# Convolution taps on GpSimd: block 1 off TensorE, block 2 and the 64 last channels of blocks 2 and 3 off VectorE

## The chip, the cores and the metric

The kernel runs on one core of a Trainium2 chip. The metric is device time in microseconds (us) of one launch; lower is better. Five engines work side by side, each with its own queue that it empties in order: TensorE (PE in the rows, with its weight loads as PEld), VectorE (DVE), ScalarE (ACT), GpSimd (POOL) and SyncE (SP), which here issues nearly all transfers. An instruction waits until the semaphores that it names are high enough, and everything behind it on its engine waits with it.

## What is computed

Tokens (2 sequences of 4096, 192 channels) go through a causal convolution of 7 taps along the sequence, whose weights are a softmax over the taps and shared by the 24 channels of a head, then through two layers of the same form with different activations:

```python
out[b, s, c] = sum_k softmax(weight)[head(c), k] * x_pad[b, s + k, c]      # 7 taps
h = x @ w_in;  g = where(h >= 1, h, where(h <= -1, 0, (h + 1)**2 / 4));  x = g @ w_out
h = x @ w_in2; g = h * sigmoid(1.702 * h);                               out = g @ w_out2
```

with 192 x 2048 and 2048 x 192 weights in each layer.

## The kernel before, in words

Activations lie channels by tokens. The 8192 tokens are cut into 16 blocks of T = 512 tokens; a block has 128 first channels (tile `xt0`, part 0) and 64 last channels. The last channels of two neighbouring blocks share one tile of 128 partitions (`xt1`, part 1), so the convolution of part 1 is done for blocks 2j and 2j+1 at once. Matrix products run in fp32r with each operand split in a high and a low half: `split` (L72 to L74) lets ACT copy the high half and DVE subtract it to get the low one. The names are `xah`, `xal` for the halves of the 128 first channels of a block, `xb` for both halves of the last 64, `ghi`, `glo` for the halves of a hidden tile, `wt` for the weights.

The weights come as fp64 words (`raw`) and are turned into fp32 halves on the chip by `weight_ops` (L101): per tile of 128 hidden units, ACT makes `wa` (L117), DVE takes bits (L118) and joins them (L122) into `wd`, ACT copies the high half (L127), DVE makes the low halves (L131, L132). Layer 1 has 16 such tiles, f = 0 to 15.

Work is cut into units (phase, f), one hidden tile of one block and layer each, taken in an order written out by hand (`units`): f = 0 to 3 of block 0, then of block 1, then 4 to 7 of block 0, and so on, then block 2, and so on. A step issues the first product of unit u on PE (`gemm1`, L237, five matmuls), its activation on ACT and DVE (`act_a`, L265: two ACT instructions and one DVE instruction for layer 1), the split of the unit before (`act_b`, L279), and the second product of the unit four steps back (`gemm2`, L300, five matmuls). The first 48 steps run this way; after them two units are run together on the two halves of the PE array (`both`). Everything else is hung on steps by the dictionary `plan`: `at(step, op)` appends, and `beside(step)` emits it behind the step's own instructions. So every engine's order is fixed when the program is built.

The convolution is done in three ways in the kernel before.

- `conv_taps` (L148): seven DVE instructions of 128x512, the first a multiply (L152), the others a multiply-add (L153). Block 0's first channels (`cva`, before step 0) and all of blocks 2 to 15 go this way. For the pair j = 1 (blocks 2 and 3) one DVE instruction is hung on each of steps 10 to 25: seven taps of block 2's first channels, `put_a` (its split), seven taps of part 1 (`cvb`), `put_b`.
- `conv_on_pe` (L163): seven diagonal matrices of 128x128 (`diag`) are made, and seven fp32 matmuls add the taps up in PSUM. Part 1 of blocks 0 and 1 goes this way, with diagonals from ACT, into `cb_ps`.
- The same with diagonals from GpSimd: block 1's 128 first channels, into `ca_ps`. Its seven matmuls are hung on steps 0 to 2 behind `gemm1`; the split into `xah`, `xal` follows at step 2, and step 4 is the first that reads them.

The pool `o_p` (tag `o`, two buffers) holds the diagonals here, and output tiles much later.

Of the kernel before, what the change touches and what calls it, by code (L numbers as in the profile page):

```python
# [8 lines left out]
F32 = mybir.dt.float32  # L9
# [6 lines left out]
P = 128  # L16
T = 512
# [3 lines left out]
def kernel(  # L21
# [21 lines left out]
    nc = tc.nc  # L43
# [104 lines left out]
    def conv_taps(part, t, c):  # L148
        def tap(k):
            w, x = taps[:, part, k : k + 1], t[:, k : k + T]  # L150
            if k == 0:
                return lambda: nc.vector.tensor_scalar_mul(c, x, w)  # L152
            return lambda: nc.vector.scalar_tensor_tensor(c, x, w, c, op0=ALU.mult, op1=ALU.add)  # L153

        return [tap(k) for k in range(K)]

    def warm_up():

        w = bank(7, "warm")
        for _ in range(9):  # L160
            nc.tensor.matmul(w[:, 0:P], ident, ident, start=True, stop=True)
# [12 lines left out]
    def put_a(i, c):  # L174
        split(c, *x1[i][:2])
# [5 lines left out]
    def put_b(i, c):  # L181

        b, halved = i % B, phases.index((1, i)) * NF >= WHOLE
        t = x1[i][2 + (b if halved else 0)]
        hi, lo = (t[0:DB], t[DB:P]) if b == 0 else (t[DB:P], t[0:DB])
        split(c[b * DB : (b + 1) * DB], hi, lo)
        if halved:
            swap_halves(x1[i][3 - b], t)

    def conv_ops(j):  # L190

        ta, tb = xt[0, B * j], xt[1, j]
        ca = cv_p.tile([P, T], F32, tag="cva", name="cva")
        cb = cv_p.tile([P, T], F32, tag="cvb", name="cvb", bufs=1)
        x1[B * j] = new_xs()
        ops = conv_taps(0, ta, ca) + [lambda: put_a(B * j, ca)]
        ops += conv_taps(1, tb, cb) + [lambda: put_b(B * j, cb)]
        st = {}

        def begin():  # L200
            st["c"] = cv_p.tile([P, T], F32, tag="cva", name="cva")
            x1[B * j + 1] = new_xs()
            st["ops"] = conv_taps(0, xt[0, B * j + 1], st["c"])
            put_b(B * j + 1, cb)

        ops.append(begin)
        ops += [lambda: st["ops"].pop(0)() for _ in range(K)] + [lambda: put_a(B * j + 1, st["c"])]
        return ops
# [215 lines left out]
    def conv_at(j):  # L424
        first, second = (unit_at[phases.index((1, B * j + k)), 0] for k in range(B))
        ops = []
        at(first - 30, lambda: fetch_x((0, B * j), (1, j), (0, B * j + 1)))
        at(first - 22, lambda: ops.extend(conv_ops(j)))
        for k in range(2 * (K + 1)):
            at(first - 22 + k, lambda: ops.pop(0)())  # L430
        for k in range(K + 2):
            at(second - 16 + k, lambda: ops.pop(0)())

    with tc.manual_schedule():
        nc.sync.dma_start(taps, taps_in)
# [11 lines left out]
        for i in range(B):  # L447
            x1[i] = new_xs()
        ca = cv_p.tile([P, T], F32, tag="cva", name="cva")
        cb_ps, ca_ps = bank(3, "cb_ps"), bank(2, "ca_ps")  # L450
        a0 = conv_taps(0, xt[0, 0], ca)
        b_ops = conv_on_pe(1, xt[1, 0], cb_ps, ident, nc.scalar.mul)
        a1 = conv_on_pe(0, xt[0, 1], ca_ps, ident, nc.gpsimd.tensor_scalar_mul)
        for op in b_ops:
            op()

        ws = [weight_ops(1, f, raw.pop((1, f))) for f in range(CH - 1)]
        order = a0[0:3] + ws[0][0:1] + a0[3:5] + ws[0][1:3] + a0[5:7] + ws[0][3:4] + ws[1][0:1]
        order += [lambda: put_a(0, ca)] + ws[1][1:2] + [lambda: put_b(0, cb_ps)] + ws[1][2:] + ws[2]
        for op in order:  # L460
            op()
        fetch_w(1, 3)
        for k, op in enumerate(weights_at(1, 3)):
            at(k // 2, op)
        for k, op in enumerate(a1):
            at((k + 2) // 3, op)
        at(1, lambda: put_b(1, cb_ps))
        at(2, lambda: put_a(1, ca_ps))

        def convert_at(n, f, steps):  # L470
            at(steps[0] - 3, lambda: fetch_w(n, f))
# [108 lines left out]
```

## Time and profile before

| | us |
|---|---|
| median of 3 runs | 1138.7 (1138.65 to 1138.96) |
| the profiled execution, whole | 1138.51 |
| its span, first to last instruction | 1136.7 |
| PE busy in the span | 1127.7 (99%) |
| ACT busy | 823.0 (72%) |
| DVE busy | 713.6 (63%) |
| POOL busy | 6.7 (1%) |

The shares are means over the span. They say that PE is nearly always at work, but a PE row's end is modelled, so a PE that waits briefly between two matmuls can still look busy; there the distance between the starts of two matmuls tells more. The beginning (up to about 80 us) is different from the rest: there the weights of layer 1 are converted and the convolutions of the first blocks are done.

### The profile page before, as it was taken

What the parts mean: (1) busy time and instruction counts of PE and PEld (TensorE: products, weight loads), DVE (VectorE), ACT (ScalarE), POOL (GpSimd) and SP (SyncE); (2) the same over time, 40 slices, a digit from 0 to 9 for tenths busy, and PEclk for the clock granted to TensorE, in tenths of its full rate; (3) what the DMA queues carried; (4) which work ended last, traced back from release to release, by engine and by line L of the source; (5) the groups of instructions that cost most, each with busy time, mean ns of one, the idle gap of its engine ahead of it and who ended that gap; (6) DMA issues with size and microseconds to landing.
All of it is one profiled execution on the core that took longest, in us unless ns stands there. A gap on an engine that the chain in (4) does not pass through costs nothing.

```text
span 1136.7 us, 22822 instructions
## 1 busy us (share of the span) xinstructions
PE 1127.7 (99%) x9324; PEld 927.1 (82%) x9324; DVE 713.6 (63%) x1152; ACT 823.0 (72%) x1468; POOL 6.7 (1%) x13
## 2 busy tenths in 40 slices
PE   9999999999999999999999999999999999999998
PEld 5878888888888888888888888888888888888886
DVE  7998765675557756476564756647566575655532
ACT  7989875867758677686776768677586776868654
POOL 2000000000000000000000000000000000000000
PEclk9999999999999999999999999999999999999999
DMA  5321420100001000010000100010000100000000
GB/s 176 124 65 43 123 76 11 57 10 25 10 11 43 17 18 10 11 43 20 15 19 12 33 20 15 20 43 1 20 15 20 44 1 20 15 20 15 11 15 14
DMA packets 16680, 36.40 MB, mean 32 GB/s; under 512 B 2497, under 2 KB 2753, under 8 KB 16577
## 3 DMA queue, kind: packets, MB, share of 16 engines
q1 hardware_dynamic: 16432, 34.82, 10.4%
q8 instruction: 73, 1.20, 0.5%
q14 instruction: 31, 0.25, 0.1%
q10 hardware_dynamic: 144, 0.13, 0.0%
HBM read 21.05 MB, written 6.29 MB: 24 GB/s over the span
## 4 chain that ended last, share of the span: by engine, by line
PE 94%; DVE 3%; ACT 2%; issue 1%; DMA 0%; SPq 0%
PE acc L361 46%; PE h L361 42%; PE acc L315 3%; PE h L250 3%; DVE glo L74 1%; DVE a L274 1%; PE ca_ps L170 1%; DVE wd L122 0%; DVE cva L153 0%; DMA raw<-in_w_dram 0%; ACT a L273 0%; ACT a L272 0%; ACT wa L117 0%; ACT wt L127 0%; DVE wt L131 0%
## 5 line engine op out<-in xcount | busy, mean ns | idle before, releaser
L361 PE MATMUL acc<-ghi,wt 64*128 64x512 f32 x2772 | 835.1, 386 | 0.0
L361 PE MATMUL h<-xah,wt 64*128 64x512 f32 x1848 | 713.6, 386 | 0.0
L361 PE MATMUL acc<-glo,wt 64*128 64x512 f32 x1848 | 678.0, 386 | 0.0
L361 PEld LDWEIGHTS acc<-ghi,wt 64*128 64x128 f32 x2772 | 468.5, 184 | 53.9 <-ACT ghi L73 0.3
L74 DVE TENSOR_TENSOR glo<-a,ghi 128x512 fp32r<-128x512 f32 x512 | 341.3, 688 | 232.9 <-ACT ghi L73 223.6
L361 PEld LDWEIGHTS acc<-glo,wt 64*128 64x128 f32 x1848 | 340.0, 184 | 36.5 <-DVE glo L74 0.8
L361 PEld LDWEIGHTS h<-xah,wt 64*128 64x128 f32 x1848 | 340.0, 184 | 36.2 <-issue 0.4
L361 PE MATMUL h<-xal,wt 64*128 64x512 f32 x924 | 356.8, 386 | 0.0
L73 ACT CAST ghi<-a 128x512 fp32r<-128x512 f32 x512 | 301.3, 614 | 26.2 <-DVE a L274 25.7
L274 DVE SCALAR_TENSOR_TENSOR a<-h,a 128x512 f32<-128x512 f32 x256 | 176.8, 690 | 159.7 <-ACT a L273 159.4
L276 ACT ACTIVATE a<-h 128x512 f32<-128x512 f32 x256 | 150.8, 596 | 153.9 <-PE h L361 146.0
L361 PE MATMUL h<-xb,wt 64*128 64x512 f32 x693 | 230.9, 386 | 0.0
L361 PE MATMUL h<-xc,wt 64*128 64x512 f32 x693 | 230.7, 386 | 0.0
L272 ACT ACTIVATE a<-h 128x512 f32<-128x512 f32 x256 | 151.0, 590 | 53.0 <-PE h L361 52.3
L361 PEld LDWEIGHTS h<-xal,wt 64*128 64x128 f32 x924 | 170.0, 184 | 17.9
L273 ACT ACTIVATE a<-a 128x512 f32<-128x512 f32 x256 | 161.8, 632 | 8.2
L361 PEld LDWEIGHTS h<-xc,wt 64*128 64x128 f32 x693 | 127.5, 184 | 17.9
L361 PEld LDWEIGHTS h<-xb,wt 64*128 64x128 f32 x693 | 127.4, 184 | 9.0
L153 DVE SCALAR_TENSOR_TENSOR cva<-xt,taps,cva 128x512 f32<-128x512 f32 x90 | 67.2, 747 | 1.3
L250 PE MATMUL h<-xah,wt 128*128 128x512 f32 x100 | 40.5, 405 | 2.6 <-DVE wt L131 2.6
L315 PE MATMUL acc<-ghi,wt 128*128 128x512 f32 x150 | 42.4, 390 | 0.0
L315 PEld LDWEIGHTS acc<-ghi,wt 128*128 128x128 f32 x150 | 28.1, 188 | 6.2 <-issue 0.4
(61 smaller groups left out, 455.3 us busy)
## 6 DMA issues: line engine op xcount, KB each, us to landing
raw<-in_w_dram SPq DMA_DIRECT2D x32, 448.0 KB, 3.4
xc<-xb SPq DMA_DIRECT2D x44, 128.0 KB, 2.2
xt<-in_xa_dram SPq DMA_DIRECT2D x16, 259.0 KB, 3.5
out_dram<-o SPq DMA_DIRECT2D x15, 256.0 KB, 2.0
out_dram<-o SPq DMA_DIRECT2D x17, 128.0 KB, 2.3
xt<-in_xb_dram SPq DMA_DIRECT2D x8, 259.0 KB, 3.2
xb<-xc SPq DMA_DIRECT2D x14, 128.0 KB, 2.2
out_dram<-o ACTq DMA_DIRECT2D x1, 128.0 KB, 1.8
```

The source lines that it names most:

```text
L73: nc.scalar.copy(hi, src)
L74: nc.vector.tensor_sub(lo, src, f32(hi))
L153: return lambda: nc.vector.scalar_tensor_tensor(c, x, w, c, op0=ALU.mult, op1=ALU.add)
L170: return lambda: nc.tensor.matmul(c, d[:, k], t[:, k : k + T], start=k == 0, stop=k == K - 1)
L250: nc.tensor.matmul(h, w, r, start=j == 0, stop=j == len(prods) - 1)
L272: nc.scalar.activation(a, h, AF.Relu, bias=0.5, scale=0.5)
L273: nc.scalar.activation(a, a, AF.Square)
L274: nc.vector.scalar_tensor_tensor(a, h, 1.0, a, op0=ALU.max, op1=ALU.min)
L276: nc.scalar.activation(a, h, AF.Gelu_apprx_sigmoid)
L315: nc.tensor.matmul(acc, w, r, start=id(acc) in fresh, stop=last and ends[id(acc)] == k)
L361: mm = nc.tensor.matmul(banks[n], w, r, start=n in fresh, stop=ends.get(n) == k)
```

## The change

GpSimd gets a convolution of its own, `conv_taps_aside`: for each tap a multiply by the tap's weight and an add, where the multiply may be done by ACT. Block 1's first channels are multiplied by ACT (seven instructions, put between the weight instructions ahead of step 0) and added up by GpSimd (six adds), in SBUF; its seven matmuls on PE and its seven diagonals go. For j = 1, block 2's first channels and part 1 of blocks 2 and 3 are both multiplied and added by GpSimd (14 multiplies, 12 adds); block 3's first channels stay on DVE. The products lie in buffers `y` of the pool `o_p`.

```diff
+    def conv_taps_aside(part, t, c, mul=nc.gpsimd.tensor_scalar_mul):
+        def tap(k):
+            w, x = taps[:, part, k : k + 1], t[:, k : k + T]
+
+            def op():
+                if k == 0:
+                    mul(c, x, w)
+                else:
+                    y = o_p.tile([P, T], F32, tag="o", name="y")
+                    mul(y, x, w)
+                    nc.gpsimd.tensor_add(c, c, y)
+
+            return op
+
+        return [tap(k) for k in range(K)]
...
-        ops = conv_taps(0, ta, ca) + [lambda: put_a(B * j, ca)]
-        ops += conv_taps(1, tb, cb) + [lambda: put_b(B * j, cb)]
+        conv = conv_taps_aside if j == 1 else conv_taps
+        ops = conv(0, ta, ca) + [lambda: put_a(B * j, ca)]
+        ops += conv(1, tb, cb) + [lambda: put_b(B * j, cb)]
...
-        at(first - 30, lambda: fetch_x((0, B * j), (1, j), (0, B * j + 1)))
-        at(first - 22, lambda: ops.extend(conv_ops(j)))
-        for k in range(2 * (K + 1)):
-            at(first - 22 + k, lambda: ops.pop(0)())
+        if j == 1:
+            steps = [*range(4, 4 + K), 17, *range(5 + K, 5 + 2 * K), 25]
+            at(1, lambda: fetch_x((0, B * j), (1, j)))
+            at(20, lambda: fetch_x((0, B * j + 1)))
...
-        cb_ps, ca_ps = bank(3, "cb_ps"), bank(2, "ca_ps")
+        cb_ps = bank(3, "cb_ps")
+        ca1 = cv_p.tile([P, T], F32, tag="cva", name="cva")
...
-        a1 = conv_on_pe(0, xt[0, 1], ca_ps, ident, nc.gpsimd.tensor_scalar_mul)
+        a1 = conv_taps_aside(0, xt[0, 1], ca1, nc.scalar.mul)
...
-        order += [lambda: put_a(0, ca)] + ws[1][1:2] + [lambda: put_b(0, cb_ps)] + ws[1][2:] + ws[2]
+        order += a1[0:2] + [lambda: put_a(0, ca)] + a1[2:3] + ws[1][1:2] + [lambda: put_b(0, cb_ps)] + a1[3:4] + ws[1][2:3]
+        order += a1[4:6] + ws[1][3:] + ws[2][0:1] + a1[6:] + ws[2][1:]
...
-        for k, op in enumerate(a1):
-            at((k + 2) // 3, op)
...
-        at(2, lambda: put_a(1, ca_ps))
+        at(2, lambda: put_a(1, ca1))
```

The splits of block 2 stay hung on steps 17 and 25. The fetch of its inputs moves from step 2 to step 1, and that of block 3's first channels to step 20.

On ACT, ahead of step 0, this stands in the program before (behind the diagonals; `Pool_49` and its like are the engines' semaphores, `DMAHW` those of transfers):

```order
L117 ACTIVATE wa<-raw 128x448 [waits DMAHW4_49]
L73 CAST xah<-cva 128x512 [waits DVE_49]
L73 CAST xb<-cb_ps 64x512 [waits PE_49]
L127 CAST wt_88<-wd 128x448 [waits DVE_49]
L117 ACTIVATE wa<-raw 128x448 [waits DMAHW6_49,Activation_49]
L127 CAST wt_88<-wd 128x448 [waits DVE_49]
L272 ACTIVATE a<-h_201 128x512 [waits PE_49]
```

In the changed program the same place on ACT reads:

```order
L117 ACTIVATE wa<-raw 128x448 [waits DMAHW4_49]
L163 ACTIVATE cva<-xt,taps 128x512 [waits DMAHW5_49]
L166 ACTIVATE y<-xt,taps 128x512
L73 CAST xah<-cva 128x512 [waits DVE_49]
L166 ACTIVATE y<-xt,taps 128x512 [waits Pool_49]
L73 CAST xb<-cb_ps 64x512 [waits PE_49]
L166 ACTIVATE y<-xt,taps 128x512 [waits Pool_49]
L127 CAST wt_88<-wd 128x448 [waits DVE_49]
L166 ACTIVATE y<-xt,taps 128x512
L166 ACTIVATE y<-xt,taps 128x512 [waits Pool_49]
L117 ACTIVATE wa<-raw 128x448 [waits DMAHW6_49]
L166 ACTIVATE y<-xt,taps 128x512 [waits Pool_49]
```

Seven multiplies have come between the weight instructions and the splits of block 0, and four of the six that write `y` wait for GpSimd.

On GpSimd, from the making of the identity matrix to the end, this is the program before:

```order
masks.py:197 MEMSET ident 128x128
masks.py:199 ISA
masks.py:199 AFFINE_SELECT ident<-ident 128x128
L167 TENSOR_SCALAR diag<-ident,taps 128x128 x7
L573 UNCONDITIONAL_BRANCH
L573 ISA
```

The changed program has this on GpSimd from the same place on (the last pair of rows then goes on alike to six adds, and again to six for `cvb`):

```order
masks.py:199 AFFINE_SELECT ident<-ident 128x128
L167 TENSOR_TENSOR cva<-cva,y 128x512 x6
L163 TENSOR_SCALAR cva<-xt,taps 128x512
L166 TENSOR_SCALAR y<-xt,taps 128x512
L167 TENSOR_TENSOR cva<-cva,y 128x512
L166 TENSOR_SCALAR y<-xt,taps 128x512
L167 TENSOR_TENSOR cva<-cva,y 128x512
```

Seven narrow multiplies have gone, and 32 instructions of 512 columns have come.

On DVE, in steps 10 to 12, the program before reads (`a` is the activation, `h` the hidden tile in PSUM):

```order
L274 SCALAR_TENSOR_TENSOR a<-h_452,a 128x512
L74 TENSOR_TENSOR glo<-a,ghi 128x512
L131 TENSOR_TENSOR wt_88<-wd,wt_88 128x384
L132 TENSOR_TENSOR wt_88<-wd,wt_88 128x64
L122 SCALAR_TENSOR_TENSOR wd<-wa,wd 128x448
L152 TENSOR_SCALAR cva<-xt,taps 128x512
L274 SCALAR_TENSOR_TENSOR a<-h_483,a 128x512
L74 TENSOR_TENSOR glo<-a,ghi 128x512
L118 TENSOR_SCALAR wd<-raw 128x448
L153 SCALAR_TENSOR_TENSOR cva<-xt,taps,cva 128x512
```

In the changed program DVE has there:

```order
L291 SCALAR_TENSOR_TENSOR a<-h_476,a 128x512
L74 TENSOR_TENSOR glo<-a,ghi 128x512
L131 TENSOR_TENSOR wt_88<-wd,wt_88 128x384
L132 TENSOR_TENSOR wt_88<-wd,wt_88 128x64
L122 SCALAR_TENSOR_TENSOR wd<-wa,wd 128x448
L291 SCALAR_TENSOR_TENSOR a<-h_503,a 128x512
L74 TENSOR_TENSOR glo<-a,ghi 128x512
L118 TENSOR_SCALAR wd<-raw 128x448
```

One convolution instruction a step has gone from DVE; the others stand in their old order.

## Rows read from the trace of the kernel before

**Rows 1.** The page: engines over the span, and chain that ended last.
```profile
PE 1127.7 (99%) x9324; PEld 927.1 (82%) x9324; DVE 713.6 (63%) x1152; ACT 823.0 (72%) x1468; POOL 6.7 (1%) x13
...
PE 94%; DVE 3%; ACT 2%; issue 1%; DMA 0%; SPq 0%
```

**Rows 2.** Stretches: us, busy (instructions) of PE, PEld, DVE, ACT, POOL, clock, DMA, GB/s.
```profile
24.00:40.00 16.00, 16.00 (x71) 13.24 (x71) 14.36 (x31) 15.46 (x30) 0.00 (x0) 1.00 0.59 195
40.00:60.00 20.00, 18.97 (x84) 15.38 (x83) 19.20 (x39) 17.43 (x33) 0.00 (x0) 1.00 0.31 93
60.00:80.00 20.00, 18.40 (x81) 14.72 (x80) 19.95 (x40) 17.11 (x33) 0.00 (x0) 1.00 0.21 69
```

**Rows 3.** PE in order of time, around two waits: start, us, what, idle before.
```profile
57.25 0.61 PE L315 MATMUL acc<-glo,wt 128*128 128x512 f32 x2
58.90 0.50 PE L250 MATMUL h<-xah,wt 128*128 128x512 f32 x1 [1.03 <-DVE wt L131]
...
76.75 0.73 PE L315 MATMUL acc<-glo,wt 128*128 128x512 f32 x2
79.08 0.50 PE L250 MATMUL h<-xah,wt 128*128 128x512 f32 x1 [1.60 <-DVE wt L131]
```

**Rows 4.** The chain that ended last: start, us, what.
```profile
16.10 2.58 PE ca_ps L170 x6
...
83.92 1.13 PE h L250 x5
85.06 1.13 PE acc L315 x5
```

**Rows 5.** ACT ahead of step 0 in order of time, and where block 1 is split.
```profile
4.63 2.14 ACT L167 ACTIVATE diag<-ident,taps 128x128 f32<-128x128 f32 x7
...
9.11 0.57 ACT L127 CAST wt<-wd 128x448 fp32r<-128x448 f32 x1 [1.82 <-DVE wd L122]
9.58 0.62 ACT L117 ACTIVATE wa<-raw 128x448 f32<-128x448 f32 x1
...
22.43 0.59 ACT L73 CAST xah<-ca_ps 128x512 fp32r<-128x512 f32 x1 [0.57 <-PE ca_ps L170]
```

**Rows 6.** Stretches (as rows 2): from block 0's split to block 1's; the end.
```profile
10.59:22.43 11.84, 10.97 (x32) 5.68 (x31) 10.19 (x22) 8.88 (x16) 0.00 (x0) 1.00 0.39 117
1134.00:1137.00 3.00, 0.00 (x0) 0.00 (x0) 0.00 (x0) 0.00 (x0) 0.00 (x0) 0.63 0.39 112
```

**Rows 7.** ACT up to 80 us, by form: busy, mean ns of one, idle before.
```profile
L273 ACT ACTIVATE a<-a 128x512 f32<-128x512 f32 x26 | 16.4, 632 | 0.8
```

**Rows 8.** GpSimd's multiplies (one line of the code): ns min/median/max, first and last start.
```profile
L167 POOL TENSOR_SCALAR diag<-ident,taps x7: 794/807/1260, 4.2 to 9.4; 128x128 f32<-128x128 f32 x7
```

**Rows 9.** GpSimd and DVE side by side in order of time: start, us, what.
```profile
6.97 0.78 DVE L153 SCALAR_TENSOR_TENSOR cva<-xt,taps,cva 128x512 f32<-128x512 f32 x1
7.43 0.79 POOL L167 TENSOR_SCALAR diag<-ident,taps 128x128 f32<-128x128 f32 x1
7.79 0.75 DVE L153 SCALAR_TENSOR_TENSOR cva<-xt,taps,cva 128x512 f32<-128x512 f32 x1
8.20 1.26 POOL L167 TENSOR_SCALAR diag<-ident,taps 128x128 f32<-128x128 f32 x1
8.46 0.62 DVE L122 SCALAR_TENSOR_TENSOR wd<-wa,wd 128x448 uint32<-128x448 uint32 x1
8.99 0.78 DVE L153 SCALAR_TENSOR_TENSOR cva<-xt,taps,cva 128x512 f32<-128x512 f32 x1
```

**Rows 10.** DVE over one pair of steps: start, us, what.
```profile
48.57 0.61 DVE L122 SCALAR_TENSOR_TENSOR wd<-wa,wd 128x448 uint32<-128x448 uint32 x1
49.11 0.74 DVE L153 SCALAR_TENSOR_TENSOR cva<-xt,taps,cva 128x512 f32<-128x512 f32 x1
49.77 0.68 DVE L274 SCALAR_TENSOR_TENSOR a<-h,a 128x512 f32<-128x512 f32 x1
...
53.74 0.61 DVE L122 SCALAR_TENSOR_TENSOR wd<-wa,wd 128x448 uint32<-128x448 uint32 x1
```

More of the change, by code (lines that the diff above doesn't have):

```diff
@@ L426, in conv_at @@
         ops = []
-        at(first - 30, lambda: fetch_x((0, B * j), (1, j), (0, B * j + 1)))
-        at(first - 22, lambda: ops.extend(conv_ops(j)))
-        for k in range(2 * (K + 1)):
-            at(first - 22 + k, lambda: ops.pop(0)())
+        if j == 1:
+            steps = [*range(4, 4 + K), 17, *range(5 + K, 5 + 2 * K), 25]
+            at(1, lambda: fetch_x((0, B * j), (1, j)))
+            at(20, lambda: fetch_x((0, B * j + 1)))
+        else:
+            steps = range(first - 22, first - 22 + 2 * (K + 1))
+            at(first - 30, lambda: fetch_x((0, B * j), (1, j), (0, B * j + 1)))
+        at(steps[0], lambda: ops.extend(conv_ops(j)))
+        for k, step in enumerate(steps):
+            at(step, lambda k=k: ops[k]())
         for k in range(K + 2):
-            at(second - 16 + k, lambda: ops.pop(0)())
+            at(second - 16 + k, lambda k=k: ops[2 * (K + 1) + k]())
     with tc.manual_schedule():
```

## The prediction

> **What bounds the kernel now.** I read the page first: PE is busy for 99% of the span and makes 94% of the chain that ended last [rows 1]. So, looked at as a whole, only what PE issues or waits for counts. Then the chain in order of time: from 79 us to the end it is matmuls alone, ten in a step, 1.13 + 1.13 = 2.27 us a step [rows 4]. A change that ends before that point is worth just what it moves the start of that solid part.
>
> Ahead of it the stretches show others at the limit: ACT busy 15.46 of 16 us from 24 to 40, DVE 19.20 of 20 and 19.95 of 20 from 40 to 80 [rows 2]. PE pays in two places, both waiting for weights that DVE finishes (L131): the second matmul of the pair at 57.25 starts 0.23 later and the next one only at 58.90, and the same at 76.75 and 79.08 [rows 3]. Start to start, less the 0.23 of a running matmul, that is 1.2 + 1.7 = 2.9 us. Why DVE is late is seen in its order: from one `wd` to the next, a pair of steps, it needs 53.74 - 48.57 = 5.17 us, where PE takes 2 x 2.27 = 4.53 [rows 4, 10]. It falls back by 0.64 us a pair.
>
> **What goes.** (a) Seven fp32 matmuls into `ca_ps`, recorded as 14 passes; six passes take 2.58 us [rows 4], so 14 take 6.0 us of PE in steps 0 to 2. (b) Two convolution instructions per pair of steps on DVE, each 49.77 - 49.11 = 0.66 us [rows 10]. DVE's pair then costs 5.17 - 1.32 = 3.85 us, under PE's 4.53: if nothing else touches DVE, both waits of PE go, -2.9 us.
>
> (a) saves less than its 6.0 us. Step 4 reads block 1's split, so it cannot start before ACT's `xah` at 22.43 [rows 5], and ACT's queue now carries the convolution. Before, ACT's 16 instructions from 10.59 to 22.43 were 8.88 us of work [rows 6]. Now ACT may start its first multiply behind `wa` of 9.58, at 10.1: instructions of 0.57 follow each other after 0.47 [rows 5], so I take 0.1 off each that waits for nothing. A multiply of 128x512 is not in the trace. Below is 0.31 us, the seven narrow ones' 2.14 / 7, if width were free; above is four times that, 1.22 [rows 5]. I take 0.63, the square, which also goes from SBUF to SBUF with 512 columns [rows 7], and 0.53 from start to start. Seven make 3.7 us. So if GpSimd cost nothing, `xah` would come at 10.1 + 8.9 + 3.7 = 22.7, that is 0.3 us later than before, although PE has lost 6.0 us of work.
>
> **The adds in that queue.** Of the six products `y`, the second, third, fifth and sixth wait for an add (the order rows), and everything behind them on ACT waits too: the weights' copies, so DVE's low halves, so PE's steps 1 to 3. How long is an add of 128x512? The nearest rows are GpSimd's multiplies of 128x128: 0.794 to 1.260 us, median 0.807 [rows 8]. They end in step with DVE: one ends at 8.22, 0.47 behind the end of DVE's 6.97 instruction (7.75); the long one ends at 9.46, again 0.47 behind the moment (8.99) at which the next DVE instruction follows `wd`. It had been issued at 8.20 and sat through all of `wd` [rows 9]. So GpSimd waits until DVE lets go of something. DVE pays a little too: its instructions of 6.97 and 8.99, which follow without a gap, take 0.78 us, that of 7.79 takes 0.75 [rows 9]; with the 0.09 by which 8.99 overlaps the end of `wd` (9.08) a narrow multiply holds DVE up for about 0.11 us per 128 columns of input. This is an estimate from those rows.
>
> Bounds of an add: 0.8 us if width is free, 4 x 0.8 = 3.2 if all of it scales. Mine, nearer to the row that it is built from: 0.73 for a narrow multiply without its wait, and 7 more inputs of 128 columns at 0.11, 1.5 us; a wide multiply, 3 more, 1.06 us.
>
> Now the chain, with d for an add: `y` of the first tap is ready at 11.3; then add, product, add, product, add, add until the sixth product may start: 11.3 + 4d + 2 x 0.65 = 12.6 + 4d. Without waits it would start at 10.1 + 6 x 0.53 + 4 x 0.5 = 15.3 (four other ACT instructions stand before it). Delay 4d - 2.7: 3.3 us for d = 1.5, 0.5 for 0.8, 10.1 for 3.2. With the 0.3 above, step 4 starts **3.6 us later**, and ACT, full from 24 to 40 [rows 2], hands that on.
>
> The Trainium skill ("GPSIMD Engine Reference", section 3.1, Elementwise — side-by-side cycle accounting) states 4497 ns for a two-input add of 2048 columns; a quarter, 1.12 us, would be an estimate for 512 and make the delay 1.8 in place of 3.3, the end 1.5 us earlier. No run here shows it.
>
> **What GpSimd does to DVE.** From block 2's inputs on (I put them at 28 us: fetched at step 1, behind the weights' transfers) GpSimd runs 14 wide multiplies and 12 adds without waiting for any step: 14 x 1.06 + 12 x 1.5 = 32.8 us of its own, some 38 with its waits, until about 66 us. Bounds of what DVE loses: nothing (no row has DVE wait more than 0.03 us), or at each of the 26 the whole time that the inputs are held, 4 x 0.11 = 0.44 for a multiply and 0.88 for an add, 16.7 us. I go by the order of a pair of steps: of DVE's seven gaps two are followed by the activation `a`, which reads the hidden tile from PSUM, and 0.6 us of holding is free there; in the other five the next instruction has its inputs in SBUF and stands. The mean hold is 0.64; 5/7 of that and 2/7 of the adds' overhang (0.13) make 0.50 us, times 26, 13.0 us. DVE has 4.53 - 3.85 = 0.68 us to spare per pair, 8.4 pairs in 38 us, 5.7 us. It falls back by 7.3. Before, it fell back by 0.64 over the 8 pairs of steps 10 to 25, 5.1, and PE lost 2.9: 2.2 were taken up by buffers. So PE loses 7.3 - 2.2 = **5.1 us**; from 0 to 8.8 by the bounds.
>
> What DVE does when GpSimd holds on is hardly in these rows, so the rule matters: the Trainium skill ("SBUF — State Buffer", section Who interferes with whom) says that DVE with two SBUF inputs and a GpSimd instruction that reads SBUF share a read port, and whoever starts second stands until the first is through. That GpSimd stands, the trace agrees (8.20 to 9.46); that DVE stands for a whole wide add, no run here shows yet.
>
> **Sum.** The profiled execution took 1138.51, its span 1136.7; the 1.8 around it stay. 1138.5 + 3.6 - 2.9 + 5.1 = **1144.3 us**; the median of the runs, 1138.7, is 0.2 off and within their spread.
>
> Costed at nothing: SP's earlier fetch for blocks 2 and 3 and the late one of block 3 (steps 1 and 20, used from step 48 on); the third `cva` buffer in turn; the splits at steps 17 and 25, since GpSimd has its first 13 instructions done some 19 us after 28 and step 17 comes at about 27 + 13 x 2.27 = 56. If the splits had to wait, ACT would stand and PE with it (third rival).
>
> **Rivals.**
> 1. DVE does not stand. For it: its instructions beside GpSimd lost at most 0.03 us [rows 9]. Against: GpSimd's own wait of 0.5 us shows that something is shared. Then 1138.5 + 3.6 - 2.9 = 1139.2, no change that can be told. Chance 0.22.
> 2. Faster: GpSimd adds in 0.7 us or less and DVE does not stand. ACT then hardly waits, the start costs 0.3 and the two waits of PE go: 1138.5 + 0.3 - 2.9 = 1135.9. For it: PE does lose 6.0 us of work and DVE 10 us. Against: the narrow multiply alone takes 0.79. It decides itself at d = 0.7 (4d = 2.7) and with DVE's standing under 8 us. Chance 0.10.
> 3. GpSimd is too slow for its dates: at 2.2 us and more for each of the 26, the first 13 end after step 17 and the last after step 25; ACT stands at `xah`. At 3.2 us each 41.6 us for 13, 13 late at the first date and about as much again at the second, so 1138.5 + 10.1 - 2.9 + 26 = 1171.7. For it: nothing shows that width is cheap. Chance 0.07.
> 4. The granted clock falls. PE issues 20 matmuls from 12 to 27 us, in groups some 3 us apart; after its last matmul the clock's mean over 3 us is 0.63 [rows 6], while through the waits of 1.2 and 1.7 us it stayed 1.00 [rows 2]. At the lower level (1.2 GHz) a step takes 4.53 in place of 2.27 us; two such steps add 4.5, less what ACT delays anyway: about 1147. The Trainium skill ("TensorE: Matmul & The Clock Gate", Part 1) says that an idle PE falls to half its rate. Chance 0.08.
>
> The forecast keeps 0.53. A measurement of this kernel tells about 0.2% (2.3 us) from no change. Slower: nearly all of the forecast (0.50) and rivals 3 and 4, 0.65. Same: 0.22, most of rival 1 and the forecast's low edge. Faster: rival 2 and a little of rival 1, 0.13. The range of 8 in 10 reaches from just above rival 2 to the upper bound of DVE's loss with adds of 2 us (1138.5 + 5.6 - 2.9 + 8.8 = 1150.0) and a little of rival 4 on top: 1136.5 to 1152. The forecast's own range is 1140 to 1150.
>
> **What the next profile must show.** `xah` of block 1 on ACT at about 26 us in place of 22.43, with four products before it waiting for GpSimd; adds of about 1.5 us. From 28 to 66 us GpSimd busy, and DVE's instructions with SBUF inputs longer or later by about 0.5 us for each of its 26; `a` unchanged. PE waiting for `wt` between 35 and 72 us by some 5 us, and matmuls alone on the chain after that. Clock 1.00 throughout. I am wrong if PE's starts have no gap after step 4 (rival 1), if `xah` comes by 23 (rival 2), or if splits on steps 17 and 25 are what ACT waits for (rival 3).

## The result and the profile after

The changed kernel takes 1153.5 us (median of 4 runs, 1151.8 to 1154.4) against 1138.7 (1138.5 to 1139.0) for the kernel before: 1.26% slower, ratio 1.0126 with a 95% interval of 1.0114 to 1.0138. The prediction was 1144.3 with a range up to 1152. Its sign was right and the two costs that it named, a late start and DVE standing beside GpSimd, both came; but it gave 5.6 us of a loss of 14.8.

The profiled execution took 1153.45 us, its span 1151.7. On the page PE's chain still has 94%, as in [rows 1], and GpSimd's time has gone from 6.7 to 52.7 us:

```profile
PE 1132.1 (98%) x9310; PEld 929.2 (81%) x9310; DVE 723.2 (63%) x1138; ACT 828.4 (72%) x1475; POOL 52.7 (5%) x38
...
PE 94%; DVE 3%; ACT 1%; issue 1%; DMA 0%; POOL 0%; SPq 0%; DVEq 0%
```

DVE was freed of 14 convolution instructions, ten us of work, and yet is busy for nearly 10 us more (723.2 against 713.6). The first pair of units run together (`both`) starts at 146.37 in place of 131.45, 14.9 us later: all of the loss lies ahead of it. The stretches, with the columns of [rows 2], show where:

```profile
24.00:40.00 16.00, 14.74 (x52) 11.38 (x52) 15.49 (x24) 13.73 (x26) 12.59 (x8) 0.77 0.45 148
40.00:60.00 20.00, 15.90 (x67) 12.02 (x66) 19.90 (x29) 13.50 (x25) 19.58 (x12) 1.00 0.23 69
60.00:80.00 20.00, 16.73 (x58) 12.15 (x57) 18.05 (x31) 15.80 (x31) 11.43 (x8) 0.83 0.34 106
...
21.00:31.50 10.50, 8.63 (x19) 5.89 (x20) 9.77 (x18) 10.06 (x19) 4.40 (x4) 0.51 0.43 138
72.50:79.50 7.00, 6.44 (x16) 5.10 (x17) 6.36 (x15) 6.29 (x13) 0.00 (x0) 0.53 0.44 156
```

From 40 to 60 us DVE is full with 29 instructions; before it was 39 in 19.20 us. Two stretches have a clock near 0.5, the lower of its two levels (1.2 GHz): there the busy shares of PE look high because each matmul takes longer.

PE in order of time, as in [rows 3]. The old waits at 58.90 and 79.08 are gone, and there are others for the same line L131:

```profile
40.48 0.61 PE L332 MATMUL acc<-glo,wt 128*128 128x512 f32 x2
42.85 0.50 PE L267 MATMUL h<-xah,wt 128*128 128x512 f32 x1 [1.76 <-DVE wt L131]
...
46.74 0.50 PE L267 MATMUL h<-xah,wt 128*128 128x512 f32 x1 [1.32 <-DVE wt L131]
...
50.34 0.49 PE L267 MATMUL h<-xah,wt 128*128 128x512 f32 x1 [1.02 <-DVE wt L131]
...
73.06 0.79 PE L267 MATMUL h<-xah,wt 128*128 128x512 f32 x1 [2.11 <-DVE wt L131]
```

What DVE does just ahead of such a wait, with GpSimd beside it (both engines in order of time; compare the durations with [rows 10]):

```profile
40.59 0.68 DVE L74 TENSOR_TENSOR glo<-a,ghi 128x512 fp32r<-128x512 f32 x1
40.78 1.60 POOL L167 TENSOR_TENSOR cva<-cva,y 128x512 f32<-128x512 f32 x1
41.19 1.61 DVE L131 TENSOR_TENSOR wt<-wd,wt 128x384 fp32r<-128x384 f32 x1
42.37 1.92 POOL L166 TENSOR_SCALAR y<-xt,taps 128x512 f32<-128x512 f32 x1
42.72 0.21 DVE L132 TENSOR_TENSOR wt<-wd,wt 128x64 fp32r<-128x64 f32 x1
42.86 1.03 DVE L122 SCALAR_TENSOR_TENSOR wd<-wa,wd 128x448 uint32<-128x448 uint32 x1
```

L131 takes 1.61 us instead of 0.55: it is issued while an add runs and ends 0.4 behind it. L122, beside a multiply, takes 1.03 instead of 0.61. PE's matmul of 42.85 stands for that L131.

GpSimd by form from 27 to 75 us, which answers the bounds from [rows 8] (count, busy, mean ns of one, idle before):

```profile
L166 POOL TENSOR_SCALAR y<-xt,taps 128x512 f32<-128x512 f32 x12 | 23.0, 1915 | 0.0
L167 POOL TENSOR_TENSOR cva<-cva,y 128x512 f32<-128x512 f32 x6 | 8.6, 1435 | 0.5
L167 POOL TENSOR_TENSOR cvb<-cvb,y 128x512 f32<-128x512 f32 x6 | 7.9, 1322 | 0.5
```

And the start: ACT's queue, as in [rows 5]. Four multiplies wait for GpSimd, then a copy waits for DVE, and `xah` of block 1 comes at 26.71 in place of 22.43:

```profile
10.10 0.70 ACT L166 ACTIVATE y<-xt,taps 128x512 f32<-128x512 f32 x1
...
12.18 0.72 ACT L166 ACTIVATE y<-xt,taps 128x512 f32<-128x512 f32 x1 [0.88 <-POOL cva L167]
...
14.40 0.72 ACT L166 ACTIVATE y<-xt,taps 128x512 f32<-128x512 f32 x1 [1.02 <-POOL cva L167]
...
16.50 0.72 ACT L166 ACTIVATE y<-xt,taps 128x512 f32<-128x512 f32 x1 [0.30 <-POOL cva L167]
...
18.06 0.72 ACT L166 ACTIVATE y<-xt,taps 128x512 f32<-128x512 f32 x1 [0.34 <-POOL cva L167]
20.06 0.56 ACT L127 CAST wt<-wd 128x448 fp32r<-128x448 f32 x1 [1.27 <-DVE wd L122]
...
26.71 0.61 ACT L73 CAST xah<-cva 128x512 fp32r<-128x512 f32 x1
```

### The profile page after: what moved, and what is told of

Its sections match the earlier page's. It is cut to its first block, busy times and chain, and to the rows that moved or that the text cites. A ratio compares the mean times of both kernels' runs of the same rounds, so it can differ in the third digit from the quotient of the medians.

```text
span 1151.7 us, 22825 instructions
## 1 busy us (share of the span) xinstructions
PE 1132.1 (98%) x9310; PEld 929.2 (81%) x9310; DVE 723.2 (63%) x1138; ACT 828.4 (72%) x1475; POOL 52.7 (5%) x38
## 4 chain that ended last, share of the span: by engine, by line
PE 94%; DVE 3%; ACT 1%; issue 1%; DMA 0%; POOL 0%; SPq 0%; DVEq 0%
PE acc L378 45%; PE h L378 41%; PE h L267 4%; PE acc L332 4%; DVE glo L74 1%; DVE wd L122 1%; DVE wt L132 0%; DVE a L291 0%; DVE wt L131 0%; ACT wt L127 0%; ACT a L290 0%; ACT a L289 0%; DVE cva L153 0%; DMA xt<-in_xa_dram 0%; POOL cva L167 0%
## 5 line engine op out<-in xcount | busy, mean ns | idle before, releaser
L378 PE MATMUL h<-xah,wt 64*128 64x512 f32 x1848 | 713.6, 386 | 0.0
L74 DVE TENSOR_TENSOR glo<-a,ghi 128x512 fp32r<-128x512 f32 x512 | 344.9, 695 | 232.7 <-ACT ghi L73 223.5
L73 ACT CAST ghi<-a 128x512 fp32r<-128x512 f32 x512 | 301.3, 614 | 26.6 <-DVE a L291 26.1
L291 DVE SCALAR_TENSOR_TENSOR a<-h,a 128x512 f32<-128x512 f32 x256 | 176.8, 691 | 163.7 <-ACT a L290 163.3
L153 DVE SCALAR_TENSOR_TENSOR cva<-xt,taps,cva 128x512 f32<-128x512 f32 x84 | 62.8, 747 | 1.3
L267 PEld LDWEIGHTS h<-xah,wt 128*128 128x128 f32 x100 | 20.0, 200 | 20.3 <-DVE wt L131 14.0
```

Source lines behind the costliest of these rows:

```text
L73: nc.scalar.copy(hi, src)
L74: nc.vector.tensor_sub(lo, src, f32(hi))
L267: nc.tensor.matmul(h, w, r, start=j == 0, stop=j == len(prods) - 1)
L291: nc.vector.scalar_tensor_tensor(a, h, 1.0, a, op0=ALU.max, op1=ALU.min)
L378: mm = nc.tensor.matmul(banks[n], w, r, start=n in fresh, stop=ends.get(n) == k)
```

## DVE's account over steps 5 to 19

A measure that most experiments below use. From the first matmul of step 5 to that of step 19 are 14 steps, 14 x 2.267 = 31.74 us for PE alone. Before, they lasted from 25.97 to 58.90 (1.19 lost); after, from 31.83 to 73.06 (9.49 lost). DVE does the work of a step some us behind PE, so its side is taken between its own instructions, from the activation `a` of step 5 to that of step 19. Before, these two start 3.73 and 6.18 us behind PE's step, in the change 3.99 and 5.80:

```profile
29.70 0.69 DVE L274 SCALAR_TENSOR_TENSOR a<-h,a 128x512 f32<-128x512 f32 x1 [0.51 <-ACT a L273]
...
65.08 0.68 DVE L274 SCALAR_TENSOR_TENSOR a<-h,a 128x512 f32<-128x512 f32 x1
```

```profile
35.82 0.68 DVE L291 SCALAR_TENSOR_TENSOR a<-h,a 128x512 f32<-128x512 f32 x1
...
78.86 0.68 DVE L291 SCALAR_TENSOR_TENSOR a<-h,a 128x512 f32<-128x512 f32 x1
```

The two stretches, with the columns of [rows 2], before and after; under each its first part, up to `a` of step 9:

```profile
29.70:65.08 35.38, 34.35 (x152) 28.14 (x151) 34.29 (x71) 31.98 (x60) 0.00 (x0) 1.00 0.36 112
29.70:39.47 9.77, 9.77 (x45) 8.10 (x44) 9.53 (x22) 9.44 (x18) 0.00 (x0) 1.00 0.51 169
```

```profile
35.82:78.86 43.04, 35.68 (x138) 26.68 (x137) 40.99 (x63) 30.66 (x57) 35.11 (x21) 0.92 0.30 92
35.82:51.29 15.47, 11.38 (x48) 8.45 (x47) 15.47 (x22) 8.40 (x16) 15.14 (x9) 1.00 0.29 90
```

and DVE's instructions by form in each whole stretch, first before:

```profile
L274 DVE SCALAR_TENSOR_TENSOR a<-h,a 128x512 f32<-128x512 f32 x15 | 10.2, 682 | 1.6 <-ACT a L273 1.6
L74 DVE TENSOR_TENSOR glo<-a,ghi 128x512 fp32r<-128x512 f32 x14 | 9.5, 677 | 0.0
L131 DVE TENSOR_TENSOR wt<-wd,wt 128x384 fp32r<-128x384 f32 x9 | 4.9, 549 | 0.0
L122 DVE SCALAR_TENSOR_TENSOR wd<-wa,wd 128x448 uint32<-128x448 uint32 x8 | 4.9, 615 | 0.0
...
L118 DVE TENSOR_SCALAR wd<-raw 128x448 uint32<-128x448 uint32 x7 | 2.7, 382 | 0.0
L132 DVE TENSOR_TENSOR wt<-wd,wt 128x64 fp32r<-128x64 f32 x9 | 1.9, 216 | 0.0
```

```profile
L74 DVE TENSOR_TENSOR glo<-a,ghi 128x512 fp32r<-128x512 f32 x14 | 12.7, 908 | 0.0
L291 DVE SCALAR_TENSOR_TENSOR a<-h,a 128x512 f32<-128x512 f32 x14 | 9.6, 682 | 1.9 <-ACT a L290 1.8
L131 DVE TENSOR_TENSOR wt<-wd,wt 128x384 fp32r<-128x384 f32 x9 | 7.1, 786 | 0.0
L122 DVE SCALAR_TENSOR_TENSOR wd<-wa,wd 128x448 uint32<-128x448 uint32 x8 | 6.9, 858 | 0.0
L118 DVE TENSOR_SCALAR wd<-raw 128x448 uint32<-128x448 uint32 x8 | 5.1, 640 | 0.0
L132 DVE TENSOR_TENSOR wt<-wd,wt 128x64 fp32r<-128x64 f32 x9 | 4.9, 549 | 0.0
```

The five lines with their inputs in SBUF are longer; `a` (L274 before, L291 after), which reads the hidden tile from PSUM, is not. The two stretches hold the same work (the fifteenth `a` of the first list is the one at its end, the eighth L118 of the second began ahead of it) but for eight instructions of the convolution before, which take 4.8 us from start to start (six of 0.66, two of 0.40). So DVE's own work is 34.29 - 4.8 = 29.5 us. In the change it is busy for 40.99 with the same work: its **standing** is 11.5. It has 31.74 - 29.5 = 2.2 to **spare**, and it is **idle** for 43.04 - 40.99 = 2.05, nearly all of it waiting for ACT. Of what that makes, 5.80 - 3.99 = 1.8 are **taken up**: DVE ends that much further behind PE than it began, and PE did not wait for it. Loss of PE = standing - spare + idle - taken up = 11.5 - 2.2 + 2.05 - 1.8 = 9.5. (This is arithmetic: it says what each part is worth, the experiments say what makes it.)

The same for the runs below. The first column is the standing from 24 to 82 us, count times the difference of the means over the five lines, so it also has what lies ahead of step 5. The next three are from `a` of step 5 to `a` of step 19; the loss is busy + idle - taken up - 31.74.

| run | standing, 24 to 82 us | DVE busy | idle | taken up | loss, steps 5 to 19 |
|---|---|---|---|---|---|
| before | 0 | 34.3 | 1.1 | 2.45 | 1.2 |
| the change | 14.2 | 41.0 | 2.05 | 1.8 | 9.5 |
| pair only | 13.8 | 41.0 | 2.05 | 0.6 | 10.7 |
| pair, no adds | 4.5 | 33.6 | 2.7 | 2.3 | 2.3 |
| pair, no multiplies | 10.1 | 34.3 | 3.8 | -1.8 | 8.2 |
| pair aside later | 11.8 | 40.6 | 2.6 | 4.1 | 7.4 |
| words earlier | 15.8 | 42.5 | 0.0 | 1.7 | 9.1 |

(To within one instruction the work of these steps is the same in all runs but the first, which has the convolution besides. Without the multiplies the adds come closer together: about half of the standing lies ahead of `a` of step 5, which starts 7.6 us behind PE, and 1.8 of that is caught up by step 19.)

## The experiments

**Parts of the change.** First each half alone. In the one, blocks 2 and 3 go back to DVE:

```diff
-        conv = conv_taps_aside if j == 1 else conv_taps
+        conv = conv_taps
...
-        if j == 1:
+        if j == 0:
```

> Block 1 as in the change (ACT multiplies, GpSimd adds), the pair of blocks 2 and 3 as before (on DVE). Theory A (the loss comes from two separate places: a start 4.5 us late through ACT's waits for GpSimd, and DVE standing beside GpSimd in steps 4 to 19): this kernel pays the first alone. DVE falls back by 0.64 us a pair of steps as before, so its two waits stay; 1138.7 + 4.5 = 1143, up to 1145 if the granted clock falls between 13 and 31 us as it did in the change. Theory B (the clock in the start costs most of the 15 us): 1148 or more. Theory C (GpSimd's 26 instructions for the pair cost nothing): 1150 to 1154, since the pair would then not matter.

Measured: 1143.6 us (1143.3 to 1144.5), ratio 1.0042 [1.0028, 1.0056].

In the other, block 1 goes back to PE:

```diff
-        a1 = conv_taps_aside(0, xt[0, 1], ca1, nc.scalar.mul)
+        a1 = conv_on_pe(0, xt[0, 1], ca_ps, ident, nc.gpsimd.tensor_scalar_mul)
...
-        order += a1[0:2] + [lambda: put_a(0, ca)] + a1[2:3] + ws[1][1:2] + [lambda: put_b(0, cb_ps)] + a1[3:4] + ws[1][2:3]
-        order += a1[4:6] + ws[1][3:] + ws[2][0:1] + a1[6:] + ws[2][1:]
+        order += [lambda: put_a(0, ca)] + ws[1][1:2] + [lambda: put_b(0, cb_ps)] + ws[1][2:] + ws[2]
```

> Block 1 as before (on PE), the pair of blocks 2 and 3 as in the change (GpSimd multiplies and adds). Theory A: the start is as before, with clock 1.00; in steps 4 to 19 DVE loses about 14 us beside GpSimd, of which some 9.5 reach PE, and the 2.9 us that PE waited before go: 1138.7 + 9.5 - 2.9 = 1145, up to 1148 if PE's waits lower the clock at the end of that stretch. Theory B (clock in the start): 1137 to 1139. Theory C (GpSimd costs DVE nothing): 1136.

Measured: 1147.7 us (1147.6 to 1148.0), ratio 1.0078 [1.0064, 1.0091]. The halves cost 4.8 and 9.0 us, 13.8 of 14.8: they nearly add up, and both lose.

**Block 1 without its adds.** The run with block 1 alone, less the six adds; block 1's sum over the taps is left out.

```diff
-                    nc.gpsimd.tensor_add(c, c, y)
```

> The kernel with block 1 alone on ACT and GpSimd, and of that without GpSimd's six adds (block 1's sum is left out, so its split reads the first tap's product): ACT's seven multiplies stay. It tells whether the late start is ACT's own work or its waiting, and DVE's, for GpSimd. By the prediction's working ACT's work alone brings block 1's split 0.3 us later: 1138.5 to 1140. Rival (seven multiplies of 0.72 in place of 0.63 us, and PE's waits lower the clock, whoever causes them): 1142 to 1143.6, as with the adds.

Measured: 1139.6 us (1138.4 to 1140.8), ratio 1.0007 [0.9998, 1.0016]. ACT still does its seven multiplies, and the split is back at its old time:

```profile
22.46 0.61 ACT L73 CAST xah<-cva 128x512 fp32r<-128x512 f32 x1
```

So the start is lost to the waiting for GpSimd and to DVE beside it, not to ACT's own work; how much to each of the two, no run tells apart.

**The pair without adds, and without multiplies.** Both leave all else of the change as it is, but not the results: in the first the sums of blocks 2 and 3 are left out, in the second all of their weighting but the first taps', with the adds reading the inputs.

```diff
-        conv = conv_taps_aside if j == 1 else conv_taps
+        conv = (lambda *a: conv_taps_aside(*a, adds=False)) if j == 1 else conv_taps
```

> The change without GpSimd's 12 adds for blocks 2 and 3 (its 14 multiplies stay; block 1 is untouched; the sums of blocks 2 and 3 are left out). In the change's trace DVE's instructions beside an add were 1.0 us longer (ten of them, 10.1 us), those beside a multiply 0.34 us (twelve, 4.1 us). Theory A (DVE's standing is what PE waits for): some 4.8 us of standing are left, under the 5.1 us that DVE has to spare in steps 4 to 19, so PE's waits of steps 9 to 19 go; left is the late start: as the kernel with block 1 alone, or a little less since DVE has no convolution: 1141 to 1143.6. Rival (what counts is how long GpSimd is busy, and the multiplies are the longer part, 14 x 1.9 of 43.6 us): still 1148 or more.

```diff
+                    if muls:
+                        y = o_p.tile([P, T], F32, tag="o", name="y")
+                        mul(y, x, w)
+                        nc.gpsimd.tensor_add(c, c, y)
+                    else:
+                        nc.gpsimd.tensor_add(c, c, x)
```

> The change without GpSimd's multiplies by a tap for blocks 2 and 3 (12 adds of the inputs themselves and two first multiplies stay; the weighting of blocks 2 and 3 is left out). Theory A: 12 adds cost DVE some 12 us as before, only closer together (12 x 1.3 = 16 us, seven steps); DVE gives back what it can up to step 19: 1147 to 1151. Rival (busy time of GpSimd counts): 17 in place of 43.6 us, two fifths of the loss: 1143 to 1145.

Measured: 1144.0 us (1143.3 to 1145.6; 1.0050 [1.0034, 1.0065]) and 1149.8 (1149.5 to 1149.9; 1.0096 [1.0082, 1.0110]). The first is 0.4 above its expected range, since waits at steps 19 and 27 stayed (1.27 and 0.50 us); the second is inside. Taking away the adds gives back 9.5 us, taking away the multiplies 3.8, although the multiplies last longer. In PE's steps 5 to 19:

```profile
31.02:65.03 34.01, 32.48 (x141) 25.95 (x140) 31.60 (x60) 30.06 (x57) 22.25 (x13) 1.00 0.37 120
```

```profile
31.19:71.16 39.97, 34.08 (x142) 27.08 (x140) 36.77 (x60) 30.20 (x56) 17.02 (x12) 0.96 0.31 101
```

GpSimd is busy for 22.25 us in the first and 17.02 in the second, but DVE's standing (24 to 82 us) is 4.5 and 10.1, of 14.2 in the change. It is mostly the two-input adds that hold DVE; the multiplies hold it too, for less.

**The clock.** The change, with 35 matmuls of the identity matrix put before the first products of steps 1, 2, 3 and 19, into PSUM that is overwritten next:

```diff
+        fillers = {1: 8, 2: 12, 3: 6, 19: 9}
...
+                for _ in range(fillers[step]):
+                    nc.tensor.matmul(f_ps[:, 0:P], ident, ident, start=True, stop=True)
```

> The change, with 35 small matmuls of the identity (as in the warm-up) that nothing reads, put ahead of the first products of steps 1, 2, 3 and 19, where PE stands for weights: they keep PE at work and ought to keep the granted clock at 1.00. Theory A': the low clock costs about 2.6 us behind step 19 (13 matmuls at 0.43 instead of 0.23 us, on the path to the end) and up to 1.9 us in steps 4 and 5: 1149 to 1151. Rival: PE waits for DVE's weights anyway, so the clock costs nothing: 1153.5 as the change.

Measured: 1152.2 us (1151.8 to 1152.6), ratio 1.0117 [1.0103, 1.0130]: 1.3 us back, less than expected (1149 to 1151). The clock is whole from 13.4 to 40 us, but other waits move in: steps 5 to 19 lose 10.3 in place of 9.5 and the wait at step 27 is back (91.21 to 93.14).

```profile
13.40:40.00 26.60, 22.95 (x120) 18.75 (x121) 23.19 (x36) 22.28 (x41) 18.46 (x11) 1.00 0.38 117
```

**Where in the program GpSimd's work lies.** The pair alone, started five steps later, when a tile of weights comes only every second step:

```diff
-            steps = [*range(4, 4 + K), 17, *range(5 + K, 5 + 2 * K), 25]
-            at(1, lambda: fetch_x((0, B * j), (1, j)))
+            steps = [*range(9, 9 + K), 22, *range(10 + K, 10 + 2 * K), 30]
+            at(7, lambda: fetch_x((0, B * j), (1, j)))
```

> The run with the pair alone on GpSimd (block 1 on PE), but its inputs fetched at step 7 in place of 1 and its splits hung on steps 22 and 30 in place of 17 and 25. GpSimd's 26 instructions then lie from about 34 to 79 us in place of 22 to 67, that is out of steps 2 to 6, where DVE makes a tile of weights in every step, and partly in steps 24 to 30, where it makes none. Theory A (the step of the prediction that failed is the credit: in the early steps DVE has nothing to spare, so its standing goes straight to PE): standing about the same, 11 to 13 us, but PE loses only 13 - 0.68 x 10 pairs - 2.2 of buffers, about 4, less the 2.9 of the old waits that go: 1138.5 to 1141.5. Rival (PE loses what an add costs wherever it stands in the first 80 us, since DVE is at its limit all along): 1146 to 1148 as the run with the pair alone. If the split on step 30 waits for GpSimd, PE has one long wait at about 80 us and the time says nothing of either.

Measured: 1145.6 us (1145.5 to 1146.6), ratio 1.0063 [1.0049, 1.0076]. Both theories missed, the rival by 0.4. In steps 5 to 9 PE now loses nothing, where the pair alone lost 3.2 and the change 1.95; from 9 to 19 it loses 7.4, as the pair alone did (7.6), and the old wait at step 27 stayed. DVE fell 4.1 us further behind without PE waiting for that, the most of these runs. So leaving the crowded early steps saves 3.3 us of the pair's 10.7 (2.1 in the whole run), and not the rest.

**Whether the order of ACT and DVE spoils it.** In the change ACT stands 11.7 us for DVE's `wd`, with the next activation behind it. Here the first two pieces of the eight last weight tiles are hung a step earlier:

```diff
-            convert_at(1, f, range(s, s + 4))
+            convert_at(1, f, range(s, s + 4) if f < 2 * CH else (s - 1, s, s + 2, s + 3))
```

> The change, but for the eight weight tiles of layer 1 from f = 8 on, ACT's wa (L117) and DVE's bits and joins (L118, L122) are hung one step earlier; ACT's copy of the high half (L127), which reads DVE's wd, and DVE's low halves stay. No work is taken away, GpSimd's adds stay. Theory A (DVE's standing becomes a loss of PE because ACT stands at L127 for a late wd, 11.7 us in all between 27 and 82 us, and the next activation stands behind it): ACT's wait for wd falls to below 5 us, DVE stands as before (13 to 15 us), and the time falls by 3 to 6 us, to 1147.5 to 1150.5. Rival (DVE's own throughput is the bound, 43.4 of 45 us busy from 27 to 72, so the order does not matter): 1152.5 to 1154.

Measured: 1152.2 us (1152.1 to 1152.5), ratio 1.0119 [1.0105, 1.0133]. ACT's waits from 27 to 82 us by line, first in the change, then here (us in total, times, longest):

```profile
ACT wt L127 <- DVE wd L122: 11.7, 8, 2.6
```

```profile
ACT ghi L73 <- DVE a L291: 4.6, 8, 1.0
ACT wt L127 <- DVE wd L122: 3.7, 2, 1.9
```

8.0 us of that wait went and 4.2 of another came (L73, 0.4 in the change); the time fell by 1.3 us, 0.3 below the rival's range. From `a` of step 5 to `a` of step 19 DVE is never idle, and its standing rose to 15.8:

```profile
36.37:78.86 42.49, 35.08 (x143) 26.95 (x142) 42.49 (x64) 32.39 (x59) 36.91 (x21) 0.96 0.30 93
```

My theory falls: the order cost PE little; DVE, without any idle time, still needs 42.49 us for steps in which PE needs 31.74. The same edit in the kernel before:

> The same edit in the kernel before, as the control. There ACT waits for wd 4.2 us between 27 and 82 us, and PE waits twice, 2.9 us in all. Theory A: the wait for wd goes, but PE's two waits are DVE's throughput (5.17 us a pair of steps against PE's 4.53) and stay at 1 to 3 us: 1137 to 1139. Rival (the order of ACT and DVE makes the waits here too): both go, 1135.5 to 1136.5.

Measured: 1137.9 us (1137.5 to 1138.1), ratio 0.9991 [0.9982, 1.0000]; the two waits shrink and stay.

**The standing where DVE has time.** The kernel before, but with block 4's first channels and the 64 last ones of blocks 4 and 5 on GpSimd, in the part where two units run together:

```diff
+        conv = conv_taps_aside if j == 2 else conv_taps
...
+            s = first - 28
+            steps = [*range(s, s + K), s + 13, *range(s + 1 + K, s + 1 + 2 * K), s + 21]
```

> The kernel before, with block 1 on PE and blocks 2 and 3 on DVE, but the first channels of block 4 and the 64 last ones of blocks 4 and 5 multiplied and added by GpSimd, in the same pattern of 28 steps, in the part where two units run together and DVE has far more to spare than in the first 80 us. Theory A (DVE's standing beside GpSimd is paid only where DVE has nothing to spare): the instructions beside an add are still about 1 us longer, but PE does not wait: 1138.2 to 1139.2, no change. Rival (an add costs PE its 0.5 to 1.0 us wherever it lies, through the port or through the order of ACT and DVE behind it): 12 adds and 14 multiplies cost 5 us and more here too, 1143 or above.

Measured: 1139.2 us (1138.7 to 1139.8), ratio 1.0005 [0.9996, 1.0014]. The stretch, and DVE's low halves in it (before: x23, 688 ns):

```profile
205.00:252.00 47.00, 47.00 (x418) 38.85 (x416) 32.72 (x42) 36.49 (x65) 45.22 (x26) 1.00 0.06 17
```

```profile
L74 DVE TENSOR_TENSOR glo<-a,ghi 128x512 fp32r<-128x512 f32 x23 | 21.5, 957 | 5.0 <-ACT ghi L73 4.6
```

An L74 stands as long here, 0.27 us on average, 23 x 0.27 = 6.2 us (less in all than in the change, as the weights' lines L118 to L132 do not run here). PE has no wait at all, with 418 matmuls in the stretch against 420 before. DVE is busy for 32.72 of 47 us: where it has that much time left, its standing cost PE nothing.

**The two old waits without GpSimd.** The kernel before, with block 2's 16 DVE instructions four steps later, and then spread thinly at first and closely at the end, where the weights are done:

```diff
-        at(first - 22, lambda: ops.extend(conv_ops(j)))
+        begin = first - (18 if j == 1 else 22)
+        at(begin, lambda: ops.extend(conv_ops(j)))
```

> The kernel before, with the 16 DVE steps of the pair of blocks 2 and 3 hung on steps 14 to 29 in place of 10 to 25 and nothing else changed. If PE's two waits of 2.9 us before (steps 19 and 27) come from DVE falling back through these instructions while it also makes weights, four fewer lie ahead of either wait, 4 x 0.66 = 2.6 us, and most of the waiting goes: 1136 to 1137. Rival: the waits come from the late start of the weights, whatever DVE does besides: 1138.7. If block 2's split at step 29 is too late for step 32, PE waits there instead: 1139 or more.

```diff
+        if j == 1:
+            steps = [10, 12, 14, 16, 18, 20, 22, 24, 25, 25, 26, 26, 27, 27, 28, 29]
```

> The kernel before, with the 16 DVE steps of blocks 2 and 3 hung on steps 10, 12, ... 22, 24 and then on 25 to 29 up to two a step, so that DVE has one convolution instruction per pair of steps while it makes weights (5.17 - 0.66 = 4.51 us against PE's 4.53). Moving them by four steps took away the wait at step 19 and left 1.8 us at step 27. Here both waits ought to go: 1138.7 - 2.9 = 1135.8. Rival (the wait at step 27 comes from when the last weights are begun, not from DVE's falling back): 1137.6. If two a step are too many behind step 25, PE waits at step 32: 1138 or more.

Measured: 1137.8 us (1137.5 to 1140.3; 0.9993 [0.9984, 1.0002]) and 1137.6 (1137.3 to 1139.0; 0.9992 [0.9983, 1.0001]). Both missed their ranges. In the first only the wait at step 19 went. In the second both old waits are gone, but two new ones, 0.5 and 0.75 us, came at 112 and 131 us, both for DVE's `glo`; around the first of them ACT and DVE are both nearly full (9.66 and 9.72 of 10 us from 105 to 115). So with the weights of layer 2 wider apart as well:

```diff
-            s = 2 * NF - 1 + 9 * f // 4
+            s = 2 * NF - 2 + 5 * f // 2
```

> The kernel before with block 2's DVE steps spread over steps 10 to 29 (as the run with the pair spread), and the weights of layer 2, which ACT and DVE convert from step 31 on, a little wider apart: 5/2 steps per tile in place of 9/4. Theory A: the two waits of that run at 112 and 131 us (0.5 and 0.75 us by the starts) came because ACT is full there (19.45 of 20 us in the kernel before, and more once PE is earlier); with the weights spread they go and the time is 1136.0 to 1136.9, faster than the kernel before by about 0.2%. Rival: the waits do not come from the weights; the time stays at 1137.6, no change that can be told from that run. If the weights now come too late for layer 2 the time is over 1138.7.

Measured: 1135.8 us (1135.3 to 1136.4), ratio 0.9975 [0.9966, 0.9984]: faster than both kernels (2.7 us under the kernel before, which took 1138.5 beside it), with no work moved to GpSimd. PE's waits from 20 to 150 us, all of them (before: 2.6 us, twice):

```profile
PE acc L315 <- DVE s L377: 0.4, 1, 0.4
```

## Why the prediction was wrong

By the starts of step 5, step 19 and the first `both`:

| term | predicted | measured |
|---|---|---|
| to step 5 | +3.6 | 31.83 - 25.97 = +5.9 |
| DVE standing, steps 5 to 19 | +5.1 | +9.5 |
| old wait at step 19 | -1.2 | -1.2 |
| steps 19 to 50: old wait at step 27, and lower clock | -1.7 | 73.31 - 72.55 = +0.8 |
| sum, unrounded | +5.8 | +14.9 |

The prediction fell short by 9.2 us: 2.3 up to step 5, 4.4 in DVE's loss in steps 5 to 19, 2.5 behind step 19.

**What failed: DVE's spare time in the step "What GpSimd does to DVE", and its idle time, which had no term.** The prediction said "DVE has 4.53 - 3.85 = 0.68 us to spare per pair, 8.4 pairs in 38 us, 5.7 us". The 0.68 was read from one pair of steps with one tile of weights [rows 10] and taken for the whole stretch. But from step 5 to step 9 DVE finishes a tile in every step (four L131 in four steps): without any convolution it was busy there for 9.53 us where PE needs 4 x 2.267 = 9.07, so it had less than nothing to spare. Just there the first standing fell, 15.47 - 9.53 = 5.9 us. Over the 14 steps the spare time was 2.2: 3.5 of the 4.4 us. The other 2.05 are DVE waiting for ACT, for which the sum had nothing and gave no reason; DVE has to make up for this time like for standing. Against that, 11.5 of the standing lay in these steps in place of 13.0, and 1.8 us were taken up "by buffers" in place of 2.2. That credit came near, though not by its own working: before, DVE fell back by 34.29 + 1.09 - 31.74 = 3.64 us in these steps, of which 2.45 were taken up and PE lost 1.19; but the 0.64 a pair held no longer behind step 19, where DVE needed 18.26 us for 18.14 of PE, up to `a` of step 27. The run with the pair later bears the first part out: out of steps 5 to 9, GpSimd's work costs PE nothing there. The run with the words earlier bears out that it is DVE's total that counts: with no idle time and more standing PE lost nearly the same, 9.1.

**Right in kind, and near in size by luck: the standing.** 26 x 0.50 = 13.0 was predicted, and `a` unchanged; 14.2 was measured, and `a` is unchanged. It splits otherwise than assumed: in the change, from 27 to 74 us, ten DVE instructions that met an add lost 10.1 us together, 1.0 each, and twelve that met a multiply 4.1, 0.34 each, where the prediction had 0.88 and 0.44 as upper bounds. An add cost more than its bound and a multiply less than assumed; that the sum came so near is luck. The Trainium skill ("SBUF — State Buffer", Who interferes with whom) says that DVE with two SBUF inputs contends with a GpSimd instruction that reads SBUF; the means above agree, as does the unchanged `a`. Its rule that the first holds the shared pair for a whole instruction, stated for DVE's 2-port modes, fits an add (1.0 of 1.4 us) and not a multiply (0.34 of 1.9).

**Right in kind, sized too small: the start.** `xah` was due at about 26 and came at 26.71. Adds took 1.39 us on average (1.5 predicted), ACT's multiplies 0.72 (0.63 predicted); the rest is DVE, whose standing beside the first six adds the start's sum left out: ACT waits 1.27 us for `wd` at 20.06. Without the adds the run is within 0.9 us of the kernel before. `xah` is thus 4.3 us late, and step 4, at the lower clock (next), adds 1.6.

**The fourth rival happened, beside the forecast.** The sum had a clock of 1.00 throughout. From 13.4 to 24 us PE was busy for 5.15 of 10.6, and its matmuls ran at the lower level until 31.4; so they did again from 73.06 to 79, behind a wait of 2.11. Step 4 took 4.19 us in place of 2.58, the three steps from 19 on 9.75 in place of 6.93 before (the wait ahead of step 19 is not in either). These are about 4.4 us; the filled run, with the clock whole from 13.4 to 40, got 1.3 of them back, since waits for DVE's weights moved in. The Trainium skill ("TensorE: Matmul & The Clock Gate", Part 1) has PE fall to half its rate when idle; the level agrees (0.51 and 0.53), though PE was not idle throughout here.

**Wrong without harm: GpSimd's multiply.** 1.06 us was predicted, 1.92 measured. GpSimd needed 45 us instead of 38 and its dates at steps 17 and 25 still held: ACT waited for GpSimd for the last time at 18 us. So the third rival did not happen.

What stays open: why a multiply that lasts longer holds DVE less. A run that showed which part of it reads was not made.

## What to carry to other kernels

Work moved from a full engine to an idle one is not free if the two share something: here some 10 us of DVE's convolution, in 14 instructions, became 14.2 us of standing (27 to 74 us). Count the spare time of the engine that will stand over the same instructions from step to step, through every part that the change touches; one period does not speak for parts in which more is done. Give its idle time a term of its own. What buffers take up is read at both ends, from how far the engine's instruction of a step starts behind the same step of the engine that waits for it. The two waits that the change removed go as well when the same DVE instructions are spread over more steps, and with the weights behind them spread too that gave 2.7 us.

## What the runs showed of the hardware

- GpSimd, 128x512 fp32: an add of two tensors takes 1.27 to 1.75 us, a multiply by a value per partition 1.56 to 2.41, all beside a busy DVE: the operation with fewer inputs is the slower. The Trainium skill ("GPSIMD Engine Reference", section 4.1, Engine selection) has one-input operations at roughly line rate; the measurement differs.
- DVE's L118, with one input in SBUF, also stands beside GpSimd: 640 in place of 382 ns on average in the two stretches from `a` of step 5 to `a` of step 19.
- ACT's multiply by a value per partition takes 0.70 to 0.72 us, its square 0.63 [rows 7].
